# PE transposes for eight items' probabilities, GpSimd low parts, and divisions in pairs, in a fused attention and mixture-of-experts kernel

## The chip, the cores and the metric

The kernel runs on one core of a Trainium2 chip. The metric is device time in microseconds (us) of one execution, the median of several. TensorE (PE in the profile) multiplies matrices and writes its results to PSUM, VectorE (DVE) and ScalarE (ACT) work elementwise on SBUF and PSUM, GpSimd (POOL) works elementwise on SBUF, and SyncE (SP) issues most of the transfers.

## The reference

Three layers follow each other. The first is attention in which a query sees only the keys of its own hash bucket (6 bits of a projection); the second is a dense layer with an ELU; the third sends each token that passes a gate to one of 8 experts.

```python
# attention: B, H, S, D = 2, 8, 768, 64
mask = q_bucket[:, :, :, None] == k_bucket[:, :, None, :]
scores = where(mask, scale * q @ k.T, -1e9)
attn = exp(scores - max(scores))
attn = attn / (sum(attn) + 1e-9)
x = (attn @ v)                       # to (1536, 512)
# dense: 512 -> 2048 -> 512
h = x @ w_in
g = where(h > 0, h, exp(minimum(h, 0)) - 1)
x = g @ w_out
# experts: E = 8, 512 -> 1024 -> 512
do_compute = x @ w_skip > 0
e_idx = argmax(x @ w_gate); gate_w = softmax(x @ w_gate)[e_idx]
out = x;  out[do_compute] += gate_w * (relu(x @ w1[e_idx]) @ w2[e_idx])
```

## The kernel before, in words

Every matrix product is made from float16 operands that are split into a high part and a low part (high is the value rounded to float16, low is the rest), so one product is three: high by high, high by low, low by high.

The attention is cut into 96 items. An item is one head and one tile of 128 queries; it holds the probabilities of 128 queries against 768 keys. Items come in six groups of 16 (two query tiles of all eight heads; three groups for each batch). For item i the steps are: `qk` (TensorE: scores into PSUM tile sc), `row_max` (VectorE: nm, then the small srow and bias), `exp_p` (ScalarE: probabilities p32 in float32), `split_p` (ScalarE makes the high half of tile ph, GpSimd the low half as p32 minus high, and for every second item one DMA transpose on the SP queue turns both items' ph into pt), `pv` (TensorE: 18 products of pt with the values, sum of the row in an extra column), and, once a head's two items are through, `pv_evac` (VectorE: 1e-9 added to the sum and scaled, the reciprocal, and the product that puts a head's 64 columns into x32). After a group's last item `x_done` splits x32 in a high part (ScalarE) and a low part (VectorE) and has them transposed, on TensorE for groups 0 and 1, by DMA after that.

The dense layer of a group runs while the next group's items run: eight chunks of 512 hidden values in the first half (about 8 items: `h_mm` on TensorE, `h_exp` twice on ScalarE, `h_g` on VectorE, then `h_hi` on ScalarE and `h_lo` on VectorE, which make the two halves of tile gT from tile eh), and two output tiles in the second half (`o_mm`, and `r_*` steps for the gate, that end with a small indirect DMA that GpSimd issues into a table). Tile eh and PSUM tile h have two buffers each, ph and pt have two pairs each, and PSUM tile pv has one.

Beside the first 29 items or so, `w_piece` decodes the dense layer's weights: 32 pieces, each with three VectorE operations on tile wc, two ScalarE copies and a GpSimd subtraction (three pieces of four; the fourth has its subtraction on VectorE). After the last item the experts' weights are loaded and split (tiles estg and wt) and the experts run.

The order is a table of slots and phases: item i's scores stand in slot i, its exponential and split in slot i + 1, its `pv` in slot i + 5 (`LAG`). From that a scheduling layer makes one fixed order for each engine, and an engine carries out its own list strictly in that order.

## Time and profile before

| | |
|---|---|
| median of 3 runs | 633.02 us (631.84 to 640.87) |
| the profiled execution: time, span | 631.56 us, 629.8 us |
| busy: PE, DVE, ACT, POOL | 521.3, 469.2, 398.7, 278.1 us |
| mean granted TensorE clock | 0.898 of full speed |
| first and last exponential of an item | 39.7 and 436.6 us |

A busy time is the time in which at least one instruction of the engine ran. Matmuls overlap in it, so a busy PE need not be at its peak. The span falls into three parts: the start until the first item (0 to 40 us), the 96 items with the dense layer beside them (40 to 440 us), and the last group's dense layer with the experts (440 to 630 us).

### The profile page before, as it was taken

The numbers are of one execution on the slowest core, as the hardware profiler recorded it, in microseconds if no ns is written. First come the engines' busy times: TensorE is split into PE (matmuls) and PEld (weight loads), VectorE is DVE, ScalarE is ACT, GpSimd is POOL, SyncE is SP. The second block draws the span as 40 slices with busy tenths as digits, with TensorE's granted clock in tenths as the row PEclk, the third lists the DMA queues.
The fourth block names the chain that finished last, engine by engine and source line by source line (L and its number), as shares of the span: only waits on it lengthen the run. The fifth ranks groups of instructions, "written<-read, shape, count | busy, mean of one in ns | idle before, by whom it ended". The sixth has DMA issues, their size and how long they took to land.

```text
span 629.8 us, 13585 instructions
## 1 busy us (share of the span) xinstructions
PE 521.3 (83%) x5305; PEld 360.7 (57%) x5305; DVE 469.2 (75%) x1042; ACT 398.7 (63%) x575; POOL 278.1 (44%) x250
## 2 busy tenths in 40 slices
PE   0546646698998979999999999999978985999895
PEld 0434423476744856577657865687456534776672
DVE  4998987899864888778767876776278967789821
ACT  3767765779866766567856876578134845677610
POOL 6356765565553546445454454444085004201011
PEclk9855765588998989999999999999998986999998
DMA  7869999999795997998499759855595884999900
GB/s 257 228 191 188 246 239 237 261 219 209 159 198 111 221 185 140 201 187 150 96 162 194 130 92 157 167 101 102 92 314 165 277 290 151 324 322 351 287 27 29
DMA packets 246693, 120.56 MB, mean 191 GB/s; under 512 B 217577, under 2 KB 227945, under 8 KB 246625
## 3 DMA queue, kind: packets, MB, share of 16 engines
q1 hardware_dynamic: 244960, 116.54, 81.3%
q0 software_dynamic: 1664, 3.11, 1.5%
q8 instruction: 43, 0.70, 0.5%
q14 instruction: 26, 0.20, 0.1%
HBM read 61.90 MB, written 5.35 MB: 107 GB/s over the span
## 4 chain that ended last, share of the span: by engine, by line
PE 27%; DVE 25%; DMA 19%; ACT 17%; issue 8%; POOL 2%; SPq 0%; ACTq 0%; DVEq 0%; POOLq 0%
DMA estg<-in_moe_w_dram 7%; ACT p L450 5%; DMA pt<-ph 4%; PE ops L590 4%; PE ops L591 4%; PE ops L592 4%; PE sc L426 4%; DVE eh L565 3%; ACT ph L464 3%; DMA kT<-kn 2%; DVE nm L439 2%; ACT eh L560 2%; DVE wc L216 2%; ACT eh L559 2%; DVE wt L130 2%
## 5 line engine op out<-in xcount | busy, mean ns | idle before, releaser
L465 POOL TENSOR_TENSOR ph<-p,ph 128x768 f16<-128x768 f32 x96 | 159.4, 1661 | 136.6 <-ACT ph L464 111.2
L450 ACT ACTIVATE p<-sc,bias,srow 128x768 f32<-128x768 f32 x96 | 94.7, 986 | 51.7 <-DVE bias L443 39.4
L551 PE MATMUL hps<-xT,w_in_h 128*128 128x256 f16 x384 | 108.5, 283 | 8.3 <-DVE eh L565 7.9
L426 PE MATMUL sc<-kT,qT 128*128 128x384 f16 (+1 forms) x384 | 92.0, 366 | 20.7 <-ACT p L450 20.2
L552 PE MATMUL hps<-xT,w_in_h 128*128 128x256 f16 x384 | 108.3, 282 | 0.3 <-DVE xT L523 0.3
L553 PE MATMUL hps<-xT,w_in_l 128*128 128x256 f16 x384 | 108.3, 282 | 0.0
L439 DVE TENSOR_REDUCE nm<-sc 128x1 f32<-128x768 f32 x96 | 91.1, 949 | 9.0 <-PE sc L426 9.0
L464 ACT ACTIVATE ph<-p 128x768 f16<-128x768 f32 x96 | 81.0, 844 | 7.3 <-DMA pt<-ph 6.4
L590 PE MATMUL ops<-w_out_h,gT 128*128 128x512 f16 x192 | 74.0, 385 | 1.6 <-ACT x L609 1.4
L591 PE MATMUL ops<-w_out_l,gT 128*128 128x512 f16 x192 | 73.9, 385 | 0.0
L592 PE MATMUL ops<-w_out_h,gT 128*128 128x512 f16 x192 | 73.9, 385 | 0.0
L483 PE MATMUL pv<-vn,pt 128*128 128x65 f16 x576 | 52.3, 201 | 12.8 <-DMA pt<-ph 8.7
L483 PEld LDWEIGHTS <-pt 128*128 128x128 f16 x576 | 45.1, 103 | 24.5 <-DMA pt<-ph 11.1
L426 PEld LDWEIGHTS <-qT 128*128 128x128 f16 (+1 forms) x384 | 35.6, 106 | 40.0 <-issue 29.6
L573 ACT ACTIVATE gT<-eh 128x512 f16<-128x512 f32 x48 | 30.1, 626 | 37.6 <-DVE eh L565 37.3
L486 PE MATMUL pv<-vn,pt 128*128 128x64 f16 x576 | 52.2, 201 | 0.0
L576 DVE SCALAR_TENSOR_TENSOR gT<-eh,gT 128x512 f16<-128x512 f32 x48 | 40.1, 836 | 11.4 <-ACT gT L573 11.3
L565 DVE SCALAR_TENSOR_TENSOR eh<-hps,eh 128x512 f32<-128x512 f32 x48 | 32.9, 686 | 19.7 <-ACT eh L560 19.6
L552 PEld LDWEIGHTS <-w_in_h 128*128 128x128 f16 x384 | 38.8, 101 | 15.0 <-issue 9.2
L551 PEld LDWEIGHTS <-w_in_h 128*128 128x128 f16 x384 | 38.7, 101 | 14.6 <-issue 6.7
L130 DVE SCALAR_TENSOR_TENSOR wt<-estg,wt 128x1024 f16<-128x1024 f32 x32 | 40.9, 1295 | 7.7 <-POOL wt L127 4.7
L486 PEld LDWEIGHTS <-pt 128*128 128x128 f16 x576 | 42.5, 102 | 5.1 <-issue 0.5
(210 smaller groups left out, 1200.3 us busy)
## 6 DMA issues: line engine op xcount, KB each, us to landing
estg<-in_moe_w_dram SPq DMA_DIRECT2D x64, 512.0 KB, 5.1
wstg<-in_moe_w_in_dram SPq DMA_DIRECT2D x16, 512.0 KB, 4.8
wstg<-in_moe_w_out_dram SPq DMA_DIRECT2D x16, 512.0 KB, 5.3
qraw<-in_q_dram SPq DMA_DIRECT2D x12, 256.0 KB, 4.0
out_dram<-x SPq DMA_DIRECT2D x12, 256.0 KB, 2.4
w_out_h<-in_k_dram SPq DMA_DIRECT2D x4, 384.0 KB
raw<-in_k_dram SPq DMA_DIRECT2D x4, 384.0 KB, 5.0
raw<-in_v_dram SPq DMA_DIRECT2D x4, 384.0 KB
```

The costliest lines, as they stand in the source:

```text
L426: nc.tensor.matmul(out=ps[:, n, 0:384], lhsT=qa[0:rows_, pas, (h % QH) * GN + t, :], rhs=ka[0:rows_, pas, j * R + 3 * n:j * R + 3 * n + 3, ...
L439: nc.vector.tensor_reduce(out=nm, in_=ps[:, :, 0:384], axis=AX.XY, op=ALU.max, negate=True)
L450: nc.scalar.activation(out=p32.rearrange("p (n a) d -> p n (a d)", n=2), in_=ps[:, :, 0:384], func=AF.Exp, bias=bias, scale=srow)
L464: nc.scalar.activation(out=ph[:, 0], in_=p32, func=AF.Copy)
L465: nc.gpsimd.tensor_tensor(out=ph[:, 1], in0=p32, in1=ph[:, 0], op=ALU.subtract)
L483: nc.tensor.matmul(out=ps[:, t, 0:D + 1], lhsT=pt[:, r, :], rhs=rhs[:, D:2 * D + 1], start=(r == 0), stop=False)
L551: nc.tensor.matmul(out=ps[:, ff], lhsT=wh, rhs=xh[:, cc], start=(cc == 0), stop=False)
L552: nc.tensor.matmul(out=ps[:, ff], lhsT=wh, rhs=xl[:, cc], start=False, stop=False)
L553: nc.tensor.matmul(out=ps[:, ff], lhsT=wl, rhs=xh[:, cc], start=False, stop=(cc == CC - 1))
L590: nc.tensor.matmul(out=ps, lhsT=gh, rhs=w_out_h[:, fc], start=(fc == 0), stop=False)
L591: nc.tensor.matmul(out=ps, lhsT=gh, rhs=w_out_l[:, fc], start=False, stop=False)
L592: nc.tensor.matmul(out=ps, lhsT=gl, rhs=w_out_h[:, fc], start=False, stop=(fc == FC - 1))
```

## The change

Four edits come together. (1) For items 8 to 15 `split_p` no longer makes ph and no longer sends it through a DMA transpose. TensorE transposes the float32 probabilities themselves, in two sets of three 128x128 blocks, into PSUM tile ptp (which takes turns with the other users of PSUM tile h); ScalarE copies each set as the high part into pt, and VectorE subtracts that from PSUM and writes the low part. (2) `h_lo` moves from VectorE to GpSimd for all groups but the last, and the low part of `x_done` moves to GpSimd for all groups. For `h_lo` to be a plain subtraction the scale factors are set so that tile eh already carries gT's scale. (3) `pv_evac` runs once for a pair of heads; the PSUM tile pv holds both heads. (4) The scale factors X_S, WI_S and G_S change, all powers of two.

```diff
-X_S = 2.0**5
+X_S = 2.0**4
-WI_S = 2.0**5
-G_S = 2.0**5
+WI_S = 2.0**3
+G_S = X_S * WI_S
...
+    PPE = range(8, 16)
...
+        if i in PPE:
+
+            if j == 0:
+                pair["t"] = ap_.tile([P, 4 * R, P], F16, name="pt", tag="pt", bufs=2)
+            pt = ptile[i] = pair["t"][:, 2 * R * j:2 * R * (j + 1)]
+            for r in range(0, R, 3):
+                ps = ps_m.tile([P, 3, P], F32, name="ptp", tag="h", bufs=2)
+                for a in range(3):
+                    nc.tensor.transpose(ps[:, a], p32[:, r + a], ident)
+                hi, lo = pt[:, r:r + 3], pt[:, R + r:R + r + 3]
+                nc.scalar.copy(out=hi, in_=ps)
+                nc.vector.tensor_tensor(out=lo, in0=ps, in1=hi, op=ALU.subtract)
+            return
...
-        if t == 0:
-            pv_ps[g, h] = ps_m.tile([P, GT, D + 2], F32, name="pv", tag="pv", bufs=1)
+        if t == 0 and j == 0:
+            pv_ps[g, hp] = ps_m.tile([P, 2, GT, D + 2], F32, name="pv", tag="pv", bufs=1)
...
-        rd = ap_.tile([P, GT, 1], F32, name="rd", tag="rd", bufs=2)[:, 0:GN]
+        rd = ap_.tile([P, 2, GT, 1], F32, name="rd", tag="rd", bufs=2)[:, :, 0:GN]
...
-            nc.vector.tensor_tensor(out=xn[:, 1], in0=x[:, t], in1=xn[:, 0], op=ALU.subtract)
+            nc.gpsimd.tensor_tensor(out=xn[:, 1], in0=x[:, t], in1=xn[:, 0], op=ALU.subtract)
...
-        nc.scalar.activation(out=g_part(g, c, 0), in_=e_t[g, c], func=AF.Copy, scale=G_S * HSC)
+        nc.scalar.copy(out=g_part(g, c, 0), in_=e_t[g, c])
...
-        nc.vector.scalar_tensor_tensor(
-            out=g_part(g, c, 1), in0=e_t.pop((g, c)), scalar=G_S * HSC, in1=g_part(g, c, 0), op0=ALU.mult, op1=ALU.subtract
+        (nc.vector if g == NG - 1 else nc.gpsimd).tensor_tensor(
+            out=g_part(g, c, 1), in0=e_t.pop((g, c)), in1=g_part(g, c, 0), op=ALU.subtract
         )
...
-        if t == groups[g][2] - 1:
-            at(i + LAG, "pvevac", lambda g=g, h=h: pv_evac(g, h))
+        if t == groups[g][2] - 1 and h % 2:
+            at(i + LAG, "pvevac", lambda g=g, h=h: pv_evac(g, h // 2))
```

The scheduling layer orders all engines anew. On VectorE around items 9 to 11 the list before was this (nm, srow and bias are the maximum of an item, wc a decoded piece, rd and x the division, prq the queries' hash bits):

```order
L439 TENSOR_REDUCE nm<-sc 128x1
L216 TENSOR_SCALAR wc<-wstg 128x512
L440 TENSOR_SCALAR srow<-nm 128x1
L503 TENSOR_SCALAR rd<-pv 128x2
L219 SCALAR_TENSOR_TENSOR wc<-wstg,wc 128x512
L443 TENSOR_SCALAR bias<-nm,srow 128x1
L222 SCALAR_TENSOR_TENSOR wc<-wstg,wc 128x512
L506 RECIPROCAL rd<-rd 128x2
L369 TENSOR_REDUCE prq<-sc 128x48
L507 TENSOR_TENSOR x_694<-pv,rd 128x2x64
```

And now it is this (pt is the low part of a set of three transposed blocks, from PSUM tile ptp):

```order
L441 TENSOR_REDUCE nm<-sc 128x1
L218 TENSOR_SCALAR wc<-wstg 128x512
L474 TENSOR_TENSOR pt<-ptp,pt 128x384
L221 SCALAR_TENSOR_TENSOR wc<-wstg,wc 128x512
L474 TENSOR_TENSOR pt<-ptp,pt 128x384
L224 SCALAR_TENSOR_TENSOR wc<-wstg,wc 128x512
L442 TENSOR_SCALAR srow<-nm 128x1
L474 TENSOR_TENSOR pt<-ptp,pt 128x384
L445 TENSOR_SCALAR bias<-nm,srow 128x1
L474 TENSOR_TENSOR pt<-ptp,pt 128x384
L218 TENSOR_SCALAR wc<-wstg 128x512
```

The low parts of the items before now stand ahead of an item's bias, which its exponential waits for. When item 16's maximum comes, 21 pieces have been decoded where 18 had been; at item 28's both lists have decoded 31.

On GpSimd, in the first half of a later group (chunks of the dense layer beside eight items), the list before was this (ph is the low part of an item's probabilities, table the indirect DMA, r_pay the next tile's payload):

```order
L749 DMA table<-r_pay,r_sli 12288x2
L670 IOTA r_pay 128x1
L465 TENSOR_TENSOR ph<-p_5043,ph 128x768
L465 TENSOR_TENSOR ph<-p_5115,ph 128x768
L465 TENSOR_TENSOR ph<-p_5185,ph 128x768
L465 TENSOR_TENSOR ph<-p_5264,ph 128x768
L465 TENSOR_TENSOR ph<-p_5368,ph 128x768
L749 DMA table<-r_pay,r_sli 12288x2
```

And now, from one such DMA to the next, it is this (gT is the low part of a chunk):

```order
L769 DMA table<-r_pay,r_sli 12288x2
L690 IOTA r_pay 128x1
L480 TENSOR_TENSOR ph<-p_3950,ph 128x768
L596 TENSOR_TENSOR gT<-eh,gT 128x512
L480 TENSOR_TENSOR ph<-p_4022,ph 128x768
L596 TENSOR_TENSOR gT<-eh,gT 128x512
L480 TENSOR_TENSOR ph<-p_4088,ph 128x768
L596 TENSOR_TENSOR gT<-eh,gT 128x512
L480 TENSOR_TENSOR ph<-p_4166,ph 128x768
L596 TENSOR_TENSOR gT<-eh,gT 128x512
L480 TENSOR_TENSOR ph<-p_4270,ph 128x768
L769 DMA table<-r_pay,r_sli 12288x2
```

A chunk's low part stands between the low parts of two items, one for one.

## Rows read from the trace of the kernel before

**Rows 1.** Busy by stretch: bounds, length, PE, PEld, DVE, ACT, POOL, PEclk, DMA share, GB/s.

```profile
69.40:101.00 31.60, 17.63 (x187) 11.24 (x188) 27.05 (x64) 20.50 (x29) 20.85 (x16) 0.61 1.11 245
101.00:135.00 34.00, 25.56 (x240) 17.50 (x239) 29.70 (x68) 23.61 (x37) 19.94 (x16) 0.58 1.04 227
135.00:440.00 305.00, 288.52 (x3126) 204.28 (x3124) 230.48 (x598) 220.00 (x326) 151.94 (x120) 0.98 0.85 159
246.00:312.90 66.90, 64.11 (x698) 44.86 (x697) 51.50 (x134) 46.27 (x70) 33.32 (x28) 1.00 0.93 161
377.60:440.00 62.40, 61.76 (x668) 43.25 (x666) 44.07 (x120) 44.33 (x66) 27.95 (x20) 1.00 0.74 134
```

**Rows 2.** VectorE busy by stretch over items 8 to 27, summed.

```profile
sum 85.80, DVE 76.29; mean DVE 25.43
```

**Rows 3.** ScalarE in order of time: the exponential of item 28.

```profile
155.19 0.99 ACT L450 ACTIVATE p<-sc,bias,srow 128x768 f32<-128x768 f32 x1 [0.40 <-DVE bias L443]
```

**Rows 4.** VectorE in order of time: its two long waits, in brackets.

```profile
95.66 0.16 DVE L503 TENSOR_SCALAR rd<-pv 128x2 f32<-128x2 f32 x1 [3.21 <-PE pv L488]
...
111.77 0.69 DVE L216 TENSOR_SCALAR wc<-wstg 128x512 int32<-128x512 int32 x1 [2.94 <-ACT wf L228]
```

**Rows 5.** The chain that ended last, 85 to 111 us: start, us, what.

```profile
85.46 7.97 DMA pt<-ph
...
101.73 8.60 DMA pt<-ph
```

**Rows 6.** SyncE's queue in order of time: first and last transpose of items 8 to 15.

```profile
76.36 6.10 SPq L468 DMA_TRANSPOSE pt<-ph  x1
...
101.73 6.54 SPq L468 DMA_TRANSPOSE pt<-ph  x1
```

**Rows 7.** Groups of instructions by line: busy us, mean ns, idle before.

```profile
L465 POOL TENSOR_TENSOR ph<-p,ph 128x768 f16<-128x768 f32 x96 | 159.4, 1661 | 136.6 <-ACT ph L464 111.2 <-issue 16.4 <-DMA pt<-ph 5.6
...
L576 DVE SCALAR_TENSOR_TENSOR gT<-eh,gT 128x512 f16<-128x512 f32 x48 | 40.1, 836 | 11.4 <-ACT gT L573 11.3
...
L507 DVE TENSOR_TENSOR x<-pv,rd 128x128 f32<-128x128 f32 x48 | 13.9, 289 | 1.3
L230 POOL TENSOR_TENSOR w_in_l<-wf,w_in_h 128x512 f16<-128x512 f32 x12 | 13.8, 1154 | 12.1 <-ACT w_in_h L229 12.0
...
L517 DVE TENSOR_TENSOR xn<-x,xn 128x512 f16<-128x512 f32 x12 | 10.8, 899 | 4.8 <-ACT xn L516 4.8
...
L506 DVE RECIPROCAL rd<-rd 128x2 f32<-128x2 f32 x48 | 7.9, 164 | 1.2
...
L503 DVE TENSOR_SCALAR rd<-pv 128x2 f32<-128x2 f32 x48 | 7.4, 153 | 25.0 <-PE pv L488 24.9
```

**Rows 8.** An expert's input: float32 transposes on TensorE, then its two evacuations.

```profile
529.19 1.09 PE L917 MATMUL xgTp<-ident,xg 128*128 128x128 f32 x4 [2.25 <-DMA xg<-out_dram,idx]
...
530.31 0.60 ACT L129 ACTIVATE xgT<-xgTp 128x512 f16<-128x512 f32 x1 [1.04 <-PE xgTp L917]
...
530.94 0.69 DVE L130 SCALAR_TENSOR_TENSOR xgT<-xgTp,xgT 128x512 f16<-128x512 f32 x1
```

**Rows 9.** TensorE's waits from 135 to 440 us: total, times, longest.

```profile
PE sc L731 <- DVE r_es L671: 4.1, 1, 4.1
PE hps L551 <- DVE eh L565: 3.5, 3, 1.9
```

**Rows 10.** GpSimd and VectorE at 346.8 us, in order of time.

```profile
346.76 1.65 POOL L465 TENSOR_TENSOR ph<-p,ph 128x768 f16<-128x768 f32 x1
...
346.90 2.06 DVE L576 SCALAR_TENSOR_TENSOR gT<-eh,gT 128x512 f16<-128x512 f32 x1 [0.39 <-ACT gT L573]
```

**Rows 11.** Line L576: ns min/median/max, first and last start.

```profile
L576 DVE SCALAR_TENSOR_TENSOR gT<-eh,gT x48: 673/692/2055, 140.2 to 501.5; 128x512 f16<-128x512 f32 x48
```

**Rows 12.** The last group's low part of x, and what GpSimd starts after it.

```profile
455.16 0.69 DVE L517 TENSOR_TENSOR xn<-x,xn 128x512 f16<-128x512 f32 x1 [0.40 <-ACT xn L516]
...
456.05 3.51 POOL L892 MEMSET xg<- 128x4096 f32 x1 [15.53 <-DVE xn L517]
```

**Rows 13.** Line L749, GpSimd's indirect DMA: min/median/max ns, first and last start.

```profile
L749 POOL DMA_INDIRECT table<-r_pay,r_sli x12: 990/1038/1546, 212.0 to 538.9; - x12
```

**Rows 14.** Line L670, GpSimd's payload: its engine's idle time before it (us, times).

```profile
  DMA table<-r_pay,r_sli: 27.7, 10
```

More of the change, by code (lines that the diff above doesn't have):

```diff
@@ L474, in pv @@
         hp, j = divmod(h, 2)
-        if t == 0:
-            pv_ps[g, h] = ps_m.tile([P, GT, D + 2], F32, name="pv", tag="pv", bufs=1)
-        ps = pv_ps[g, h]
+        if t == 0 and j == 0:
+            pv_ps[g, hp] = ps_m.tile([P, 2, GT, D + 2], F32, name="pv", tag="pv", bufs=1)
+        ps = pv_ps[g, hp][:, j]
         pt = ptile.pop(i)
@@ L494, in pv, with pv_evac @@
             )
-    def pv_evac(g, h):
-        ps = pv_ps.pop((g, h))
-        if h == 0:
+    def pv_evac(g, hp):
+        ps = pv_ps.pop((g, hp))
+        if hp == 0:
             x32[g] = ap_.tile([P, GT, DM], F32, name="x32", tag="x32", bufs=1)
         GN = groups[g][2]
-        x, ps = x32[g][:, 0:GN], ps[:, 0:GN]
-        rd = ap_.tile([P, GT, 1], F32, name="rd", tag="rd", bufs=2)[:, 0:GN]
+        x, ps = x32[g][:, 0:GN, 2 * hp * D:2 * (hp + 1) * D], ps[:, :, 0:GN]
+        rd = ap_.tile([P, 2, GT, 1], F32, name="rd", tag="rd", bufs=2)[:, :, 0:GN]
         nc.vector.tensor_scalar(
-            out=rd, in0=ps[:, :, D:D + 1], scalar1=1e-9, scalar2=V_S / X_S, op0=ALU.add, op1=ALU.mult
+            out=rd, in0=ps[:, :, :, D:D + 1], scalar1=1e-9, scalar2=V_S / X_S, op0=ALU.add, op1=ALU.mult
         )
@@ L507, in pv_evac @@
         nc.vector.tensor_tensor(
-            out=x[:, :, h * D:(h + 1) * D], in0=ps[:, :, 0:D], in1=rd.to_broadcast([P, GN, D]), op=ALU.mult
+            out=x.rearrange("p t (j d) -> p j t d", j=2),
+            in0=ps[:, :, :, 0:D],
+            in1=rd.to_broadcast([P, 2, GN, D]),
+            op=ALU.mult,
         )
```

## The prediction

> **What bounds the kernel now.** I read the table of busy times first, then busy time by stretch, then the waits and the chain inside the stretches that this change touches. Over the whole span PE is busiest and DVE second, but the stretches have different limits [rows 1]. In the first two, items 8 to 15 (69.4 to 101 us) and 16 to 23 (to 135), PE is busy 17.6 of 31.6 and 25.6 of 34.0 us at a mean granted clock near 0.6 (so between its two levels, 1.2 and 2.4 GHz), while DVE has 27.1 and 29.7. From 135 us the dense layer runs beside the items, and PE is the bound: 95% over 305 us, and 99% in the last row, where DVE is at 71%.
>
> So VectorE sets the pace until about item 28: 76.3 of 85.8 us busy [rows 2], up to that item's exponential at 155.2 us [rows 3]. Of the 9.5 idle us, 6.2 are two long waits [rows 4]. The chain shows what lies behind both: a DMA transpose of probabilities, 8.0 and 8.6 us on the chain each [rows 5]. The one at 85.5 us is late for PE's `pv`; the division on DVE waits for `pv`, and the pieces queue behind the division. The one at 101.7 us holds a ph buffer that ScalarE needs, ScalarE's copy of a piece stands behind that, and DVE waits for ScalarE. Both belong to items 8 to 15, whose four transposes keep SP's queue 5 to 6.5 us each [rows 6], with a DMA share above 1 [rows 1].
>
> **Part A, up to item 28.** Removed: four DMA transposes, and eight low parts on GpSimd (1.661 us each [rows 7]). Added on VectorE: sixteen low parts of 128x384 from PSUM, 15 of them ahead of item 28's maximum. No row has that size; a 128x512 with its first input in PSUM takes 0.69 us [rows 8]. By columns that is 0.52, and 0.69 is a ceiling; I take 0.55, nearer the columns, so 15 x 0.55 = +8.2 us. Removed from VectorE by that place: 11 divisions at 0.153 + 0.164 + 0.289 = 0.606 us [rows 7] become 5 pairs. A pair's product has 256 columns; the line through 0.289 for 128 and 0.69 for 512 gives 0.42, so a pair is 0.74, and the two sums differ by 3.7 - 6.7 = -3.0. Two low parts of x, 0.899 each, go to GpSimd: -1.8. Three low parts of chunks at 0.836: -2.5. DVE's work up to item 28 changes by +0.9 us: what the transposes cost VectorE the other edits pay back. The order shows that it isn't spread evenly: by item 16 three more pieces and 13 of the low parts have been put in, so items 8 to 15 get slower and the next twelve faster.
>
> The gain must come from the waits. The 6.2 us vanish with the transposes that cause them. New waits can take their place: the low part of item i - 1 now stands ahead of item i's bias, so an exponential waits for three transposes of the item ahead (1.09 for four [rows 8]: about 0.85), a copy of 128x384 (0.60 for 512 columns: about 0.5) and a subtraction (0.55). With the exponential (0.99 [rows 3]), the bias and the steps between engines this loop is an estimated 3.5 us per item, and DVE has 27.05 / 8 = 3.4 us plus about 1 for the low parts to do in that time. DVE stays the longer by a little; I put 2 us of new waiting against it. Part A: 0.9 - 6.2 + 2 = -3.3 us. Its ends: all 9.5 us of idle time go, 0.9 - 9.5 = -8.6; or the loop costs another 0.75 us on each of eight items, 2.7. ScalarE exchanges eight copies of 768 columns for sixteen of 384 in a stretch where it is idle a third of the time [rows 1]: nothing. TensorE's 48 transposes are 48 x 0.27 = 13 us in a stretch in which it has 14 us of idle time: covered while VectorE makes that stretch longer, else it is rival 3.
>
> **Part B, item 28 to the end of the items.** Chunks, divisions and low parts of x take VectorE a further 37 x 0.836 + 10 x 0.899 + 37 x 0.606 - 19 x 0.74 = 48 us of work away, but VectorE is not what ends last. PE is: from 135 to 440 us it has 305 - 288.5 = 16.5 us without a busy instruction [rows 1]. The two longest named waits for VectorE in them are 4.1 us (a gate step queued behind other VectorE work) and 3.5 us (a chunk) [rows 9]. A lighter VectorE reaches such steps earlier. I take 3 us of the 16.5, a part of the two; ends: 8 (half of the gaps) and a loss, which is rival 2. One thing helps beside it: a low part on VectorE at 346.90 took 2.06 us because GpSimd's 1.65 us began just ahead of it [rows 10]; half of its kind take 0.69 or less [rows 11]. With the chunks' low parts on GpSimd these two no longer meet.
>
> The Trainium skill (SBUF — State Buffer, "Who interferes with whom") says why: a VectorE instruction with two SBUF inputs needs the port that GpSimd reads through, and the one that comes second waits for the whole of the other. The trace agrees in the 2.06 us. By that rule the new low part of the probabilities, with one input in PSUM, does not meet GpSimd at all, but what stays on VectorE with two SBUF inputs meets a busier GpSimd; by the one and the other the sum would stay within a microsecond or two of that without the rule.
>
> **Part C, the last group and the experts.** `h_lo` stays on VectorE here. The two low parts of x move: 1.154 (a subtraction of that shape on GpSimd [rows 7]) for 0.69 us, twice, on the path from the last item to the last group's first chunk and to the clearing of xg, which waits for them [rows 12]: +0.9 us. The last division, of a pair now, is 0.13 longer. I take +1 us, ends 0 and +3. All else after 440 us is unchanged.
>
> **The sum.** -3.3 - 3 + 1 = -5.3 on the profiled 631.56 us gives 626.3. That execution is 1.5 us under the median of 633.02, in which the three runs spread over 9 us; I forecast **626 us** for the median too.
>
> **The rivals.** 1, **VectorE was the hidden brake throughout**: all of the idle time of part A goes (-8.6) and half of PE's gaps (-8), with C at +1: 616. For it: VectorE's steps stand in every loop of an item, and it loses a tenth of its work. Against: PE at 99% in the last row of [rows 1], where no more is to be had.
>
> 2, **GpSimd becomes the bound in the first half of each group**, the slower side. There it now has, for eight items, 8 x 1.661 + 8 x 1.154 + a query preparation of some 1.3 + two indirect DMAs of 1.04 [rows 13] with 2.8 us of waiting behind each (27.7 / 10 [rows 14]): 13.3 + 9.2 + 1.3 + 7.7 = 31.5 us in a half that takes 31 to 33 (62.4 and 66.9 us for 16 items [rows 1]). If the wait behind a DMA can't be made up, an item's low part comes late, its transpose and `pv` too, and PE, which takes them in order, stands. That decides from the point where the 31.5 exceed the half's own length. One DMA with its wait is 3.9 us; one lost in each of five halves is 19.5: 631.6 - 3.3 + 19.5 + 1 = 649. Against it: the second half has none of the chunks, and `pv` lies four slots behind the split.
>
> The Trainium skill (GPSIMD Engine Reference, "3.1 Elementwise — side-by-side cycle accounting") has a rule against this edit: elementwise work stays on VectorE, because GpSimd takes 1.96 times as long for a float32 addition. The rows here give 1.154 against 0.69, 1.67 times. By the page a chunk's part would be an estimated 1.35 us and the half 33.1 us, over its length, which is this rival.
>
> 3, **the new loop and TensorE at its lower clock bind items 8 to 15**: the waits removed come back as waits for transposes. PE's 17.6 us plus 13 make 31 of the old 31.6, at a mean clock of 0.61 [rows 1]. Part A is then at its upper end, +2.7, with B at -3 and C at +1: 632, no change. For it: the low parts stand in front of the bias in VectorE's list. Against: VectorE's own work makes that stretch longer anyway.
>
> **How the numbers follow.** Forecast 0.50 (620 to 630), rival 1 0.22, rival 3 0.21, rival 2 0.07. The range must leave out no more than 0.2, so it takes in rivals 1 and 3 with some spread, 615 to 637, and leaves rival 2 outside. A change of under 2% (620.4 to 645.7) is what a measurement of this kernel can't well tell from none. Faster by more: most of rival 1 and the lowest edge of the forecast, 0.24. Slower by more: most of rival 2, 0.05. Within: 0.71.
>
> **What would show it.** Right: no wait of about 3 us on VectorE between 85 and 115 us; items 8 to 15 take 34 us or more instead of 31.6; item 28's exponential comes 2 to 5 us earlier than 155.2; PE's gaps shrink by a few us; GpSimd's busy time rises by some 45 us (40 chunks and 12 low parts of x at 1.154, less 8 at 1.661); the time after the last item grows by about 1 us. Wrong: VectorE waiting for ScalarE's copies of ptp in each item (rival 3), GpSimd above 95% in the first halves and `pv` waiting for pt there (rival 2), or every group after 246 us shorter by 3 us (rival 1). What would spoil all of it is an accident of the new order: a key or query preparation behind a GpSimd low part, between 170 and 246 us.

## The result, and the profile of the changed kernel

The change makes the kernel slower: **643.01 us** (median of 20 runs, 637.87 to 648.07) against 634.58 for the kernel before in the same runs, a ratio of 1.0141 with an interval of [1.0122, 1.016]. The profiled execution took 645.48 us, its span is 643.4 us. The profiled execution of before (631.56 us) was one of its quickest: in the experiments its median lay between 634.6 and 637.1. So where one execution is compared with one, as in the table of starts below, some 3 to 5 us are the execution and not the kernel, and what is faster or slower is taken from the ratios.

Busy time by stretch, columns as in [rows 1]: items 8 to 15, items 8 to 27, the stretch with the dense layer, and the eight chunks of a later group (its first half).

```profile
73.36:112.04 38.68, 23.71 (x221) 17.48 (x222) 36.70 (x79) 23.84 (x41) 9.26 (x9) 0.68 0.63 165
...
73.36:162.10 88.74, 61.12 (x637) 46.17 (x637) 79.89 (x171) 62.56 (x101) 44.55 (x36) 0.74 0.77 189
...
135.00:440.00 305.00, 283.67 (x3058) 201.62 (x3057) 194.47 (x495) 214.56 (x318) 200.60 (x163) 0.98 0.84 156
...
362.80:392.70 29.90, 28.86 (x332) 22.35 (x331) 17.83 (x52) 24.41 (x38) 23.38 (x20) 1.00 0.60 107
```

Items 8 to 15 take 38.7 us where they took 31.6, and VectorE is busy in 95% of them. Up to item 28 VectorE has 79.9 us of work and 8.85 us idle, where [rows 2] had 76.3 and 9.5. From 135 to 440 us VectorE has 36 us less to do than in [rows 1], and TensorE is no busier for it: 93% against 95%. (From item 28 to the last item, in each kernel's own time, it is 34.8 us less and 94% against 95%.) GpSimd is busy 78% of this first half, and 69 to 87% of the five stretches in which the chunks run.

ScalarE in order of time, the exponential of item 28 (155.19 in [rows 3]):

```profile
162.10 0.98 ACT L452 ACTIVATE p<-sc,bias,srow 128x768 f32<-128x768 f32 x1
```

VectorE in order of time: the longest wait between 60 and 125 us, and one of the new low parts:

```profile
66.58 0.96 DVE L441 TENSOR_REDUCE nm<-sc 128x1 f32<-128x768 f32 x1 [3.95 <-PE sc L428]
...
85.38 0.55 DVE L474 TENSOR_TENSOR pt<-ptp,pt 128x384 f16<-128x384 f32 x1
```

The two long waits of [rows 4] are gone. The one of 3.95 us stands before item 7's maximum, and so ahead of item 8; in the kernel before it was 0.56 us there. The chain that ended last, its longest pieces with a transpose by DMA; the two at 85 and 102 us of [rows 5] have gone, one at 56 us and two behind item 16 are on it:

```profile
56.20 7.04 DMA pt<-ph
...
121.23 7.38 DMA pt<-ph
139.00 7.22 DMA pt<-ph
```

Groups of instructions by line, columns as in [rows 7]:

```profile
L480 POOL TENSOR_TENSOR ph<-p,ph 128x768 f16<-128x768 f32 x88 | 145.9, 1658 | 75.1 <-ACT ph L479 55.2 <-issue 9.7 <-POOL gT L596 6.0
...
L596 POOL TENSOR_TENSOR gT<-eh,gT 128x512 f16<-128x512 f32 x40 | 48.0, 1201 | 9.6 <-ACT gT L592 9.3
...
L471 PE MATMUL ptp<-ident,p 128*128 128x128 f32 x48 | 10.2, 357 | 14.9 <-ACT p L452 12.4 <-DVE pt L474 2.0 <-DVE srow L442 0.5
L523 DVE TENSOR_TENSOR x<-pv,rd 128x256 f32<-128x256 f32 x24 | 10.1, 422 | 0.7
L474 DVE TENSOR_TENSOR pt<-ptp,pt 128x384 f16<-128x384 f32 x16 | 8.7, 551 | 0.0
```

The durations are near those that were estimated: 0.55 for a low part (0.55), 0.42 for a pair's product (0.42), 1.20 for a chunk's low part on GpSimd (1.154). What was not foreseen is the 12.4 us that TensorE stands before its transposes, waiting for an exponential.

GpSimd in order of time, the end of the items (answers to [rows 12]):

```profile
467.52 2.27 POOL L536 TENSOR_TENSOR xn<-x,xn 128x512 f16<-128x512 f32 x2 [11.09 <-ACT xn L535]
469.85 3.51 POOL L912 MEMSET xg<- 128x4096 f32 x1
```

From the last item's exponential (450.95) to the end of the span are 192.45 us, 0.75 less than before. And GpSimd's wait for the indirect DMA between 170 and 440 us, where the kernel before had 22.2 us in 8 cases: total, times, longest:

```profile
POOL r_pay L690 <- DMA table<-r_pay,r_sli: 12.4, 5, 3.5
```

### The profile page after: what moved, and what is told of

It reads as the page before. It is cut to its first block, busy times and chain, and to the rows that moved or that the text cites. A ratio compares the mean times of both kernels' runs of the same rounds, so it can differ in the third digit from the quotient of the medians.

```text
span 643.4 us, 13644 instructions
## 1 busy us (share of the span) xinstructions
PE 524.5 (82%) x5353; PEld 366.3 (57%) x5353; DVE 436.2 (68%) x934; ACT 399.6 (62%) x583; POOL 327.3 (51%) x294
## 4 chain that ended last, share of the span: by engine, by line
PE 31%; DVE 22%; DMA 17%; ACT 13%; issue 11%; POOL 3%; SPq 1%; ACTq 0%; DVEq 0%; POOLq 0%
DMA estg<-in_moe_w_dram 6%; PE sc L428 5%; DMA pt<-ph 4%; ACT p L452 4%; PE ops L610 3%; PE ops L611 3%; PE ops L612 3%; ACT ph L479 3%; DVE eh L584 2%; DVE nm L441 2%; DVE wt L132 2%; PE hps L570 2%; PE hps L572 2%; PE hps L571 2%; DMA x2T<-x2n 2%
## 5 line engine op out<-in xcount | busy, mean ns | idle before, releaser
L480 POOL TENSOR_TENSOR ph<-p,ph 128x768 f16<-128x768 f32 x88 | 145.9, 1658 | 75.1 <-ACT ph L479 55.2
L570 PE MATMUL hps<-xT,w_in_h 128*128 128x256 f16 x384 | 106.6, 278 | 10.4 <-DVE eh L584 7.7
L441 DVE TENSOR_REDUCE nm<-sc 128x1 f32<-128x768 f32 x96 | 91.1, 949 | 23.4 <-PE sc L428 23.4
L572 PE MATMUL hps<-xT,w_in_l 128*128 128x256 f16 x384 | 106.6, 278 | 0.0
L571 PE MATMUL hps<-xT,w_in_h 128*128 128x256 f16 x384 | 106.5, 277 | 0.0
L428 PE MATMUL sc<-kT,qT 128*128 128x384 f16 (+1 forms) x384 | 90.6, 360 | 19.3 <-ACT p L452 18.9
L479 ACT ACTIVATE ph<-p 128x768 f16<-128x768 f32 x88 | 74.3, 845 | 5.4 <-DMA pt<-ph 4.6
L596 POOL TENSOR_TENSOR gT<-eh,gT 128x512 f16<-128x512 f32 x40 | 48.0, 1201 | 9.6 <-ACT gT L592 9.3
L592 ACT CAST gT<-eh 128x512 f16<-128x512 f32 x48 | 29.5, 616 | 35.5 <-DVE eh L584 35.5
L975 POOL DMA_INDIRECT out_dram<-res,idx x8 | 13.6, 1702 | 67.9 <-DVE res L972 67.1
L570 PEld LDWEIGHTS <-w_in_h 128*128 128x128 f16 x384 | 38.2, 100 | 14.3 <-DVE eh L584 3.6
```

Of the source, the lines that this page charges most:

```text
L428: nc.tensor.matmul(out=ps[:, n, 0:384], lhsT=qa[0:rows_, pas, (h % QH) * GN + t, :], rhs=ka[0:rows_, pas, j * R + 3 * n:j * R + 3 * n + 3, ...
L441: nc.vector.tensor_reduce(out=nm, in_=ps[:, :, 0:384], axis=AX.XY, op=ALU.max, negate=True)
L479: nc.scalar.activation(out=ph[:, 0], in_=p32, func=AF.Copy)
L480: nc.gpsimd.tensor_tensor(out=ph[:, 1], in0=p32, in1=ph[:, 0], op=ALU.subtract)
L570: nc.tensor.matmul(out=ps[:, ff], lhsT=wh, rhs=xh[:, cc], start=(cc == 0), stop=False)
L571: nc.tensor.matmul(out=ps[:, ff], lhsT=wh, rhs=xl[:, cc], start=False, stop=False)
```

## The experiments

**First set: the edits apart.** e1 has only the transposes (with scales as before), e2 all but the transposes, e3 only the chunks' low parts on GpSimd, e4 only the pairs. The theory that they were to test: the transposes cost what is lost up to item 28, and the busier GpSimd what is lost from 28 to 53.

```diff
e1: PPE = range(8, 16) in the kernel before
e2: PPE = () in the changed kernel
e3, in the kernel before, with the change's scales:
-        nc.vector.scalar_tensor_tensor(
-            out=g_part(g, c, 1), in0=e_t.pop((g, c)), scalar=G_S * HSC, in1=g_part(g, c, 0), op0=ALU.mult, op1=ALU.subtract
+        (nc.vector if g == NG - 1 else nc.gpsimd).tensor_tensor(
+            out=g_part(g, c, 1), in0=e_t.pop((g, c)), in1=g_part(g, c, 0), op=ALU.subtract
e4, in the kernel before: pv, pv_evac and the "pvevac" slot of the change
```

> Only the TensorE transposes for items 8 to 15; the rest as before. Theory 1, two prices (the transposes cost some 7 us up to item 28 because their low parts lie on VectorE, which sets the pace there; the GpSimd low parts cost some 8 us between items 28 and 53): slower than before by 6 to 12 us, item 17 later by 13 us or more, item 28 by 7 or more since no division or chunk is taken off VectorE, and no further loss from item 28 to 53. Theory 2, the transposes alone through the new order: 10 us or more, with half of it after item 28. Theory 3, the GpSimd parts alone: within 2 us of before.

> The changed kernel without its transposes on TensorE: GpSimd low parts and divisions in pairs alone. Theory 1: slower than before by 5 to 8 us, with item 28 at its old time or some us earlier and the loss between items 28 and 53. Theory 2: at the time before or faster by up to 5 us. Theory 3: slower by 8 us or more.

> Only the chunks' low parts (h_lo) on GpSimd, with the scale factors that this needs; the rest as before. Theory 1 and 3: slower by 4 to 8 us, lost between items 28 and 53, where a key preparation on GpSimd stands behind low parts. Theory 2: within 2 us of before or faster.

> Only the divisions in pairs; the rest as before. All three theories: within 2 us of before, VectorE 11 us less busy. If the pair makes a head's second PSUM half wait, or an order with pv ahead of the next scores (as at item 7 of the changed kernel, 2.3 us) comes from it, slower by 2 to 5 us.

| run | median, us | ratio to before | interval |
|---|---|---|---|
| e1, transposes | 640.22 | 1.0069 | [1.0029, 1.0109] |
| e2, all but transposes | 642.90 | 1.012 | [1.0076, 1.0163] |
| e3, chunks' low parts on GpSimd | 631.43 | 0.9892 | [0.9829, 0.9956] |
| e4, pairs | 646.69 | 1.0129 | [1.0063, 1.0195] |

In these runs the kernel before had a median of 636.23 us. e3 and e4 were executed four times each; by their medians alone they would stand at 0.992 and 1.016, so their size is uncertain by some 0.3%, their sign is not.

That theory fell. Low parts on GpSimd make the kernel faster, and the edit that was costed as pure saving, the pairs, is the dearest. e1 missed its 6 to 12 us (some 4.4), and e4 cost more than was allowed for. e2 came out as the theory said, 1.2% slower, with item 28 2.4 us early and the loss behind it, but by luck: by e3 and e4 its loss comes with the pairs and not with GpSimd. The theory formed from this (called Theory 4 in the expectations): a division between a head's last `pv` and the next head's first one, in the one PSUM tile, had kept `pv` behind later scores. With one tile for two heads nothing keeps it, and the scheduling layer puts up to four items' `pv` ahead of the next scores; TensorE then stands before a pt that the DMA has not landed yet, with scores queued behind it. TensorE's list around items 1 to 3 and 8 to 11 reads, in short, `pv1 pv2 qk7 pv3` and `pv8 pv9 qk15 pv10 pv11 qk16` before, `pv1 pv2 pv3 qk7` and `pv8 pv9 pv10 pv11 qk15` in the changed kernel and in e4.

**Second set: without pairs, pairs with their order mended, transposes without VectorE's part, GpSimd's part alone.** e5 is the changed kernel with the divisions per head. e6 is e4 with a gate: one column copied on VectorE, overwritten by the `pv` behind it. e7 is e1 with the subtraction replaced by a second copy on ScalarE, so pt's low part holds the high part again and the subtraction is left out. e8 has both kinds of low parts on GpSimd, no pairs, no transposes.

```diff
e6, in e4:
+        last_bias[i] = bias
...
+        if t == 0 and i + 4 in last_bias:
+            nc.vector.tensor_copy(out=ps[:, t, D:D + 1], in_=last_bias[i + 4])
e7, in e1:
-                nc.vector.tensor_tensor(out=lo, in0=ps, in1=hi, op=ALU.subtract)
+                nc.scalar.copy(out=lo, in_=ps)
```

> The changed kernel with a division for each head as before: transposes on TensorE and all GpSimd low parts stay. Theory 4 (the pairs cost some 10 us, because without the division between two heads the order puts pv of four items in a row ahead of the next scores, and TensorE then stands before a probability tile that its DMA has not landed; the transposes cost some 4 us through VectorE; the chunks' low parts on GpSimd gain some 7): 629 to 634 us, faster than the changed kernel by 9 us or more. If the three edits hinder each other instead, 638 us or more.

> Only the divisions in pairs, as in the run of pairs alone, and a copy of 128x1 on VectorE for each head from the bias of item i + 4 into a PSUM column that pv of item i overwrites: pv of a head's first item can then not stand ahead of that bias, and the order again has the scores between the pv of items 8 to 11. Theory 4: the loss of the pairs goes, within 3 us of before, with TensorE's waits for probability tiles between 60 and 125 us back to the 8 us of before or less. If the pair's tile in PSUM or its division is the price itself, slower by 8 us or more as without the copy.

> Only the transposes for items 8 to 15, with the low part written by ScalarE as a second copy of the transposed block: the subtraction is left out, so the low part is not the rest of the rounding. VectorE is spared 16 instructions of 0.55 us. Theory 4 for the transposes (the price is VectorE's extra work): item 17 later than before by 3 us at most and item 28 at its old time or earlier, time within 2 us of before or faster. If the price is the wait for transposes and copies in the loop of an item, or the orders of other things: slower by 4 us or more as with the low part on VectorE.

> All GpSimd low parts (chunks and x), no transposes on TensorE, a division for each head. Theory 4: faster than before by 5 to 9 us, as with the chunks alone; the low parts of x on GpSimd change it by less than 2 us. If the low parts of x are late on GpSimd, 3 us or more slower than with the chunks alone.

| run | median, us | ratio to before | interval |
|---|---|---|---|
| e5, changed kernel without pairs | 638.08 | 1.0015 | [0.9971, 1.0059] |
| e6, pairs with the gate | 638.65 | 1.0043 | [1.0011, 1.0075] |
| e7, transposes, low part not subtracted | 633.14 | 0.9939 | [0.9903, 0.9975] |
| e8, GpSimd's low parts alone | 633.46 | 0.9924 | [0.9879, 0.9968] |

Taking the pairs away removes the whole loss of the change, as far as the interval of e5 tells; the 629 to 634 us expected of it were not reached (638.08, in runs in which the kernel before had 637.12). The gate takes two thirds of e4's loss away. It is not free: TensorE now waits for the copies (its waits from 60 to 130 us in e6: total, times, longest), so e6 can't show the price of a perfect order.

```profile
PE pv L487 <- DVE pv L481: 8.4, 2, 6.9
```

e7 against e1 prices VectorE's low parts. VectorE's work up to 155.2 us, first in e1, then in e7:

```profile
69.40:155.20 85.80, 60.50 (x609) 44.32 (x609) 83.15 (x183) 60.48 (x97) 39.56 (x32) 0.76 0.81 189
```

```profile
69.40:155.20 85.80, 64.11 (x714) 48.19 (x715) 80.37 (x182) 71.70 (x123) 41.95 (x33) 0.85 0.93 207
```

In e1 VectorE is busy 97% of the time in which the kernel before ran its items 8 to 27, and item 28 comes 5.3 us late. In e7, with the same transposes and more work on ScalarE, it comes 4.4 us early. The difference of 9.7 us is the sixteen low parts (16 x 0.551 = 8.8) and little else. So neither the transposes nor ScalarE's copies bind these items; the low parts on VectorE do.

**Third set: the gate in the whole change, the order alone, fewer transposes.** e9 is the changed kernel with e6's gate. e10 is the kernel before, in which only the scores of items 0 to 15 are given to the scheduling layer with priority; that moves `pv10` alone ahead of item 15's scores, `pv6 pv7` ahead of item 12's, and `pv14 pv15` ahead of item 20's. e11 has the transposes for items 8 to 11 only.

```diff
e9: as e6, in the changed kernel
e10, in the kernel before:
-                with tc.high_priority() if s >= o_end and ph in URGENT else nullcontext():
+                with tc.high_priority() if (s >= o_end and ph in URGENT) or (ph == "qk" and s < 16) else nullcontext():
e11, in e1:
-    PPE = range(8, 16)
+    PPE = range(8, 12)
```

> The whole change as it is, with one addition: a one-column VectorE copy of the bias of item i + 4 into the column that the first pv of a head then overwrites, so that this pv stands behind item i + 4's scores again, as the division between two heads had kept it. In TensorE's list pv8 pv9 pv10 pv11 qk15 becomes pv8 pv9 T13 qk15 T14 qk16 pv10 pv11. Theory 4 (the pairs cost 1.3% by the order, the transposes 0.7% by VectorE's low parts, the chunks' low parts give 1%): the copy takes about 8 us off the changed kernel, so 0.3 to 0.8% over the kernel before, 637 to 640 us, and item 28 comes within 4 us of the kernel before. Rival (the pairs' loss in the whole change is something else than order, such as the one PSUM tile held for two heads): 1.2 to 1.6% over the kernel before, 643 us or more.

> The kernel before with its divisions per head, and no other edit than that the scores of items 0 to 15 are given to the scheduling layer with high priority, which moves pv10 ahead of item 15's scores and pv6 pv7 ahead of item 12's on TensorE, a part of what the pairs' order does. Theory 4 (that order alone costs time, the pair's instructions do not): 0.3 to 1.2% slower than the kernel before, with waits of TensorE for pt of 3 us about items 6 to 11 and item 17 some 3 to 6 us later. Rival (the pair's own instructions or its PSUM tile cost the time, the order nothing): within 0.3% of the kernel before.

> The kernel before with TensorE transposes for items 8 to 11 alone, four items instead of eight. Theory 4 (VectorE's low parts at 0.55 us each are the cost; eight of them are gone against the eight-item kernel, and two DMA transposes come back): half of the loss, 0.2 to 0.5% slower, and item 28 2 to 4 us later than in the kernel before. Rival (what costs is the place where the transposes stand, or the order of pv and scores around items 12 to 15, not the number of low parts): either the whole 0.7% or nothing.

e9: 641.52 us, 1.0078 [1.0045, 1.0111]. e10: 636.4 us, 1.0013 [0.998, 1.0046]. e11: 635.37 us, 0.9983 [0.9955, 1.0012]. The gate halves the loss of the whole change, at the edge of what was expected, and item 28 is hardly earlier for it (+6.3 us against +6.9, where 4 at most was expected). e10 fell out as the rival said: these moves cost nothing that can be measured. So "any `pv` ahead of scores costs time" is refuted. It does not refute the order as a cause: up to item 20 TensorE's list in e10 is that of e4, except that in e4 `pv3` stands ahead of item 7's scores and `pv11` ahead of item 15's. If the order of these items costs e4 its time, it is at those two places. e11 missed as well: four items cost nothing, not half of eight.

**Fourth set: where the pairs cost.** TensorE's order in the changed kernel differs from that without pairs in groups 0 and 1 only. e12 has pairs in groups 2 to 5, e13 in groups 0 and 1, e14 in group 0. All else is the changed kernel. e15 is e1 for items 12 to 15.

```diff
e12, in the changed kernel (e13: (0, 1); e14: (0,)):
+    PAIRED = (2, 3, 4, 5)
...
-        if t == 0 and j == 0:
-            pv_ps[g, hp] = ps_m.tile([P, 2, GT, D + 2], F32, name="pv", tag="pv", bufs=1)
-        ps = pv_ps[g, hp][:, j]
+        w = 2 if g in PAIRED else 1
+        if t == 0 and h % w == 0:
+            pv_ps[g, h // w] = ps_m.tile([P, w, GT, D + 2], F32, name="pv", tag="pv", bufs=1)
+        ps = pv_ps[g, h // w][:, h % w]
e15, in e1:
-    PPE = range(8, 16)
+    PPE = range(12, 16)
```

> The whole change, with division in pairs in groups 2 to 5 only; groups 0 and 1 are divided head by head, so TensorE's order over items 0 to 31 is that of the changed kernel without pairs (pv2 qk7 pv3; pv8 pv9 qk15), and after that that of the changed kernel, which is the same. Theory 4 (the pairs cost by the order of the first groups): the same as the changed kernel without pairs, 0.998 to 1.006 of the kernel before. Rival (the one PSUM tile for two heads, or the division that comes only after two heads, costs in every group): 1.008 to 1.013, two thirds of the whole loss.

> The whole change, with division in pairs in groups 0 and 1 only, so the order of the first 32 items is word for word that of the changed kernel. Theory 4: all of the changed kernel's loss is here, 1.010 to 1.017 of the kernel before. Rival (cost in every group): a third of the pairs' 1.26% over the changed kernel without pairs, so 1.004 to 1.008.

> The whole change, with division in pairs in group 0 only (items 0 to 15). Theory 4, with the loss by the places where three or four pv stand ahead of scores (items 1 to 3, 8 to 11, 12 to 15, all in group 0): 1.009 to 1.016 of the kernel before. Rival (it is group 1, where the dense layer of group 0 starts beside the pairs): 0.999 to 1.005.

> The kernel before with TensorE transposes for items 12 to 15 alone. Theory (VectorE has some 9 us of idle time over items 8 to 23 in the kernel before, which takes in the low parts of four items, wherever they stand, but not of eight): as for items 8 to 11, 0.995 to 1.002 of the kernel before. Rival (items 12 to 15 are the dear place, since key and query preparation of the next group stands there): 1.004 to 1.009.

| run | median, us | ratio to before | interval |
|---|---|---|---|
| e12, pairs in groups 2 to 5 | 636.00 | 1.0021 | [0.9983, 1.0059] |
| e13, pairs in groups 0 and 1 | 644.56 | 1.0169 | [1.0095, 1.0243] |
| e14, pairs in group 0 | 642.42 | 1.0115 | [1.0041, 1.0189] |
| e15, transposes of items 12 to 15 | 638.82 | 1.0044 | [1.0004, 1.0085] |

This is the clearest result. In four groups of six pairs cost nothing (e12 is as e5), so in those neither the pair's instructions nor its one PSUM tile are dear. The first two groups carry the whole loss, and the first alone, as far as the intervals tell, the larger part of it. They are the groups in which the pairs alter TensorE's list. They are also the early groups, where VectorE sets the pace, so these runs by themselves don't separate the list from the division that comes only after two heads; e6, which keeps the pairs and gives back most of the order, keeps a third of the loss. One place can be read off. TensorE around 60 us in the changed kernel, in order of time:

```profile
59.60 0.52 PE L503 MATMUL pv<-vn,pt 128*128 128x65 f16 x6
63.28 0.24 PE L498 MATMUL pv<-vn,pt 128*128 128x65 f16 x1 [3.17 <-DMA pt<-ph]
...
64.91 0.35 PE L503 MATMUL pv<-vn,pt 128*128 128x65 f16 x3
65.07 1.47 PE L428 MATMUL sc<-kT,qT 128*128 128x384 f16 x4
```

And in e12, the same change with divisions per head here:

```profile
60.16 0.52 PE L506 MATMUL pv<-vn,pt 128*128 128x65 f16 x6
61.91 0.20 PE L501 MATMUL pv<-vn,pt 128*128 128x65 f16 x1 [1.24 <-DMA pt<-ph]
...
62.28 0.25 PE L506 MATMUL pv<-vn,pt 128*128 128x65 f16 x3
62.37 0.82 PE L430 MATMUL sc<-kT,qT 128*128 128x384 f16 x4
```

Both stand before `pv2`, whose pt is still on its way. In e12 only `pv2` stands ahead of item 7's scores, in the changed kernel `pv2` and `pv3` do; the scores start 2.7 us later. Of these, 1.4 are the later landing of pt, and 1.3 are two `pv` in place of one, with products of 0.24 us instead of 0.20. The scores then take 1.47 us instead of 0.82, TensorE's two levels. That is not the longer wait's doing: the kernel before waits 1.03 us here and takes 1.47 too.

```profile
61.11 0.23 PE L483 MATMUL pv<-vn,pt 128*128 128x65 f16 x1 [1.03 <-DMA pt<-ph]
...
61.91 1.47 PE L426 MATMUL sc<-kT,qT 128*128 128x384 f16 x4
```

Against the kernel before the scores start 3.2 us later: 0.7 because the transfer starts later, 1.5 because it lands later after its start, and 1.0 for the second `pv`. The later landing has a companion in the trace. In the changed kernel one packet of 16 KB of the queue that the profile calls "instruction" runs during the transfer (56.2 to 61.7 us, the DMA queue's row: packets, MB, share):

```profile
q8 instruction: 1, 0.02, 1.0%
```

In the first 5.5 us of this transfer such a packet stands in all eight kernels in which pt lands 7.0 to 7.2 us after the start (the seven with pairs in group 0, with the gate or without, and e1), and in none of the nine in which it lands after 5.6 to 5.7; there the next one comes 7.8 us or more after the start. So about half of what this place costs goes with that packet and not with the place of `pv3`.

Against e12, item 7's maximum comes 3.2 us later (the wait of 3.95 us on VectorE shown above), and item 8 starts 3.7 us later. In every kernel with pairs in group 0 and no gate these scores start between 64.5 and 65.6 us (e2, e4, e13, e14, the changed kernel), in the ten without between 60.8 and 62.9.

The transposes, which now stand behind that order (`qk16 T13 T14 T15 qk17`), were suspected as a second place. TensorE's waits from 60 to 125 us (total, times, longest) in the changed kernel, e14, e5 and e12, in this order:

```profile
PE ptp L471 <- ACT p L452: 12.4, 5, 3.5
```

```profile
PE ptp L473 <- ACT p L454: 12.5, 5, 3.9
```

```profile
PE ptp L471 <- ACT p L452: 5.2, 3, 2.3
```

```profile
PE ptp L473 <- ACT p L454: 4.9, 3, 2.3
```

With pairs in group 0 it is 12.4 and 12.5 us, without them 5.2 and 4.9 (and 7.7 in e1). But TensorE's waits before scores for an exponential go the other way in part (7.9, 4.9, 7.3 and 9.4 us, in the same order), and the table of starts below speaks against this place: from item 8 to item 18 the changed kernel loses 8.7 us, e14 8.7, e5 10.4 and e12 9.7. So no cost of these waits shows there.

In e4, without the transposes, the loss of the early items shows later. From 69.4 to 135 us VectorE is busy 53.1 us there and 56.8 in the kernel before, and what it does less is the decoding of weights. The 30th piece, in the kernel before and in e4, 16 us later:

```profile
145.36 0.69 DVE L216 TENSOR_SCALAR wc<-wstg 128x512 int32<-128x512 int32 x1 [0.23 <-ACT wf L228]
```

```profile
161.31 0.69 DVE L216 TENSOR_SCALAR wc<-wstg 128x512 int32<-128x512 int32 x1 [0.96 <-ACT wf L228]
```

And TensorE in e4, in order of time: the first output product of the dense layer waits for the weight that a late piece makes.

```profile
176.71 0.59 PE L594 MATMUL ops<-w_out_h,gT 128*128 128x512 f16 x1 [0.97 <-DVE w_out_l L130]
```

That wait is 1 us of the 10.3 that e4 loses from item 28 to item 49. Over these items (columns as in [rows 1]; the kernel before, then e4) TensorE stands 6.1 us longer and is busy 4.2 us longer, at a granted clock of 0.92 against 0.95. No single cause could be read from the rows.

```profile
155.19:250.85 95.66, 87.78 (x933) 61.17 (x932) 70.88 (x180) 66.21 (x97) 50.52 (x43) 0.95 0.86 165
```

```profile
159.82:265.73 105.91, 91.95 (x943) 61.84 (x943) 72.96 (x172) 68.30 (x102) 52.17 (x44) 0.92 0.86 164
```

**Starts of items.** Start of an item's exponential, less that in the kernel before (69.43, 106.39, 155.19, 250.85 and 436.6 us), in us, from one execution each:

| | item 8 | 18 | 28 | 49 | 95 |
|---|---|---|---|---|---|
| changed kernel | +3.9 | +12.6 | +6.9 | +14.1 | +14.3 |
| e1, transposes | +0.9 | +10.3 | +5.3 | +5.1 | +9.8 |
| e7, the same, no VectorE | -0.5 | -2.3 | -4.4 | -4.6 | +0.9 |
| e3, chunks on GpSimd | -0.4 | -1.0 | -2.1 | +0.1 | +2.1 |
| e4, pairs | +3.5 | +4.1 | +4.6 | +14.9 | +13.9 |
| e5, without pairs | +0.6 | +11.0 | +3.7 | +5.0 | +5.1 |
| e10, one pv moved | +0.2 | -0.4 | -4.1 | +0.2 | +5.6 |
| e11, four transposed | -1.1 | +4.4 | -0.2 | +1.7 | +3.0 |
| e12, pairs late | +0.2 | +9.9 | +2.6 | +7.1 | +6.9 |
| e14, pairs in group 0 | +4.4 | +13.1 | +5.5 | +7.7 | +8.5 |

e10 and e11, whose medians are those of the kernel before, end at +5.6 and +3.0. Their rows show how far the last column can be trusted.

## Why the prediction was wrong

**The step that failed is in part A**: "11 divisions ... become 5 pairs ... -3.0", a saving of instructions on VectorE with nothing else moved. The price of the instructions was right: from item 8 to item 28 the division's rows add up to 3.2 us instead of 5.3, so -2.1 (9 divisions became 4 pairs and the start of a fifth). But alone the pairs cost 1.29%, some 8 us. What the runs put in the step's place: each division also released the one PSUM tile between two heads, and with half of them TensorE's list changes in groups 0 and 1, where e12 to e14 place the whole loss. How much of it is the list itself stays open (below). The prediction weighs VectorE's and GpSimd's lists; TensorE's has no term in it. It named an accident of the new order as what could spoil all, but on GpSimd and between 170 and 246 us; the one that can be read off came on TensorE, ahead of item 8.

**Part A, term by term.** Forecast -3.3, measured +6.9 up to item 28. Of this 3.9 lie ahead of item 8, where the prediction had no term at all: the wait for item 7's scores. From item 8 to 28 it is 88.7 against 85.8 us, +3.0. VectorE's low parts of pt are 8.7 (8.2 forecast), chunks -2.9 (-2.5), low parts of x -1.8 (-1.8); its busy time grew by 3.6 and not by 0.9. The waits were to shrink by 4.2 us and shrank by 0.6. The two of [rows 4] did vanish, but others came, the longest for the transposed x, another for a chunk (VectorE by line from item 8 to 28, columns as in [rows 7]):

```profile
L584 DVE SCALAR_TENSOR_TENSOR eh<-hps,eh 128x512 f32<-128x512 f32 x4 | 2.7, 685 | 1.1 <-ACT eh L579 1.1
...
L542 DVE COPY xT<-xTp 128x512 f16<-128x512 f16 x2 | 0.8, 424 | 2.9 <-PE xTp L541 2.9
```

e7 shows what removing the DMA transposes is worth where nothing new stands on VectorE: from item 8 to 28 it gains 3.9 us, two thirds of the 6.2 put in.

**What held.** Items 8 to 15 take longer and the next twelve less: 38.7 and 50.1 us against 31.6 and 54.2. No wait of about 3 us stands on VectorE between 85 and 115 us. The chunks' low parts on GpSimd are worth 0.8 to 1.1% by themselves (e8, e3), 5 to 7 us; parts A and B had 4.3 and 3 for GpSimd's share. So the size of that edit was about right; where its gain falls is not shown (in e3's one profiled execution item 28 comes 2.1 us earlier and the last item 2.1 later). Rival 2 is refuted: GpSimd is busy 23.4 of 29.9 us in the first half shown above, where 31.5 were reckoned with the waits, and from 155 to 440 us no wait of TensorE is put down to GpSimd. A rule of the Trainium skill (GPSIMD Engine Reference, "3.1 Elementwise — side-by-side cycle accounting") keeps such work on VectorE. The subtraction does take longer on GpSimd, 1.201 us against 0.836 in [rows 7], but e3 is 1.1% faster with it, so here the measurement decides for GpSimd.

**Part B**, forecast -3. The ratio's 1.41% is 9.0 us; 6.9 lie ahead of item 28 and -0.75 behind the last item, so some 3 us are left, with the wrong sign, as an estimate from these numbers (7.4 between the two profiled executions). The rows give no single cause. One reading behind the forecast was wrong: the 3.5 us of [rows 9], taken for one long wait, are three, of which the longest is 1.9. **Part C** is -0.75 for +1: the two low parts of x take 2.27 us, yet the clearing of xg starts 18.9 us after the last exponential, and 19.5 before the change (456.05 in [rows 12] less 436.6).

**The other rivals.** Rival 3 said that the transposes themselves bind items 8 to 15. Waits for them did come, but e7 has all 48 of them and is 0.6% faster. What binds is VectorE, 95% busy, as the forecast had it against that rival; of the 7.1 us that these items cost, the next twelve paid back only 4.1. Rival 1, VectorE as a hidden brake throughout, is not borne out by the stretch after item 28: 34.8 us of VectorE's work are gone there and TensorE's share of busy time did not rise.

**The sum of the parts.** Transposes +0.69%, pairs +1.29%, GpSimd's low parts -0.76% make +1.2%, against 1.41 [1.22, 1.6] measured: the edits add up within their intervals.

**What stays open.** (a) The place at 60 us gives 3 to 4 us of the pairs' 8, about half of it together with the packet of (b). The rest was narrowed down to groups 0 and 1. In the table of starts it falls behind item 28, up to item 49 (+7.2 us in the changed kernel and +10.3 in e4, against +1.3 in e5 and +4.5 in e12, from one execution each), and its cause is not shown. (b) Why a packet of the instruction queue falls into the transfer of pt at 56 us in every kernel with pairs in group 0; e1 has it without pairs, and no run moves that packet by itself, so that it causes the later landing is not shown. (c) Transposes of items 8 to 11 cost nothing, of 12 to 15 0.44%, of all 0.69%. That VectorE had room for four items' low parts wherever they stand was expected and not borne out by e15; the two intervals meet, so the place is not shown either.

## What to carry to other kernels

Merging small instructions can cost more than it saves: where a scheduler makes the order, merging steps or buffers changes the lists of the engines that wait for them, so compare those lists too, above all the place of work that waits for a DMA relative to the work of the engine's other customers. Work that moves from the engine with the tightest loop to one with room (GpSimd was busy 44% of the span before) can pay off even if each instruction becomes 1.4 times as long. And price a removed wait by what the next wait in line leaves of it: of 6.2 us of long waits 3.9 came free in the best case, and 0.6 in the whole change. Of the versions run here, chunks' low parts on GpSimd alone (e3) has the lowest ratio, 0.9892 against the kernel before; with four executions it can't be told from e8 at 0.9924.

## What the runs showed of the hardware

A VectorE operation with both inputs in SBUF became longer when a GpSimd operation had begun just ahead of it. The key preparation's low part, minimum, median and maximum in ns, in the changed kernel and in the kernel before:

```profile
L290 DVE SCALAR_TENSOR_TENSOR kn<-raw,kn x4: 958/1352/1904, 187.7 to 263.5; 128x768 f16<-128x768 f32 x4
```

```profile
L288 DVE SCALAR_TENSOR_TENSOR kn<-raw,kn x4: 941/957/958, 180.5 to 251.1; 128x768 f16<-128x768 f32 x4
```

In the changed kernel two of the four, 1.90 and 1.75 us long, started 0.06 and 0.21 us behind a chunk's low part on GpSimd; the other two, with GpSimd idle, took 0.96. The one at 241.17 us, on GpSimd and on VectorE:

```profile
240.96 1.15 POOL L596 TENSOR_TENSOR gT<-eh,gT 128x512 f16<-128x512 f32 x1
```

```profile
241.17 1.75 DVE L290 SCALAR_TENSOR_TENSOR kn<-raw,kn 128x768 f16<-128x768 f32 x1
```

The rule of the Trainium skill (SBUF — State Buffer, "Who interferes with whom") that VectorE and GpSimd share a port agrees with these rows. The sixteen low parts of pt, which read one input from PSUM, took 0.547 to 0.558 us; the three of them that began while a subtraction ran on GpSimd took 0.550 to 0.555.

The same DMA transpose of two items' probabilities, of the same size, landed 5.6 us after its start in one kernel and 7.0 in another, with SP's queue held 3.7 us in both; that difference of 1.4 us is half of what the place at 60 us cost. Over 17 kernels the late landing went together with a 16 KB packet of the instruction queue that started 4.7 to 5.2 us into the transfer (8 of 8), and the early one with none in it (9 of 9).
